# Two channels on the 128 contraction rows: a long convolution beside attention on one core

## The chip, the core and the metric

The kernel runs on one core of a Trainium2 chip. The core has five engines with instruction streams of their own: TensorE (PE in the profile) multiplies matrices, VectorE (DVE) and ScalarE (ACT) work element by element, GpSimd (POOL) and SyncE (SP) here mostly clear memory and start transfers (DMAs). They wait for each other by semaphores only. Matmuls write to PSUM, which has eight banks of 128 x 512 float32 values; everything else lies in SBUF, 128 partitions wide.

The metric is the time of one execution on the device in microseconds. The kernel before takes 828.38 us, the median of three runs (827.64 to 830.67). A profile is one further execution; its page and its trace are what the prediction is read from.

## What is computed

Two independent parts share one launch, and their outputs stand side by side.

```python
def _A_ref(x, wqkv, wo):                 # x: 1 x 2048 x 512, H = 32 heads of Dh = 16
    qkv = (x @ wqkv).reshape(B, S, 3, H, Dh)
    q, k, v = ...
    scores = einsum("bhqd,bhkd->bhqk", q, k) * (Dh ** -0.5)
    o = einsum("bhqk,bhkd->bhqd", softmax(scores), v)
    return o.reshape(B, S, D) @ wo

def _B_ref(q, k, v, shift_k, ssm_k, ssm_D):   # each 1 x 2048 x 512
    k_shift = sum over t < 4 of k delayed by 3 - t times shift_k[:, 3 - t]
    kv = k_shift * v
    y = causal convolution of kv with ssm_k along S, channel by channel
    return q * (y + kv * ssm_D)

return concatenate([_A_ref(...), _B_ref(...)], axis=-1)
```

In the source the convolution is written with Fourier transforms. The kernel computes it as matrix products.

## The kernel before

**Attention.** The scores are worked through in 2048 blocks of 128 keys by 512 queries. One step of the main loop (index `T`) takes two or three blocks into PSUM banks (`qk_mm`, L728), and one instruction of ScalarE writes their exponentials to `PT` (`emit_exp`, L761). One block of some steps goes to VectorE instead, which computes the exponential in four passes (`exp_on_dve`, L803, L810 twice, L815) into `PTD`. Two steps later the value matmuls (`emit_pv`, L844) add the blocks into bank `PVB` = 6, in four groups of 32 columns of the PE array, one for each pair of heads. When a group of heads is complete, VectorE turns and normalises it (`finish_group`). The order of everything is written out in Python before launch by a planner with assumed durations: `emit_qk`, `pv_step`, `emit_bg` and `warm_up` are called in turn for each `T`, and each piece of other work is put into a step only if it is expected to end before ScalarE needs its next scores (`MARGIN`). On the device each engine just follows its list.

**Convolution.** `kv` is computed by matmuls with diagonal taps (L468) and multiplied by `v` on VectorE into the tile `KV` (L514): 128 positions on the partitions, then groups of four channels, 16 blocks of positions, and the four channels. The filter `ssm_k` is reversed and padded, stored to `kz_scratch` in device memory (`kz_store`), and read back so that each partition holds the filter shifted by one more position: a row of `WR` is such a 128 x 2048 matrix of one channel, 512 KB per load (`load_wr`, L997, issued by SP). `WR` has `R_W` = 16 rows, which makes four slots of four channels. For four channels `conv_lags` runs 16 lags; in each, four matmuls with 128 moving columns go to the four groups of 32 columns of the array (L1014). The stationary operand of lag n is the 16 - n blocks of `KV` that this distance reaches. The results of 16 channels fill bank `BGB` = 7; VectorE copies them to half of `YB` (L1028), and after 32 channels `conv_turn` transposes them on PE (8 transposes, L1039) and VectorE multiplies by `q` in the tile `QN` (L1048). When 256 channels are done, `QN` is written out.

**The planner's rules for this work.** Nothing of the convolution starts before step `N_OPEN`; until then the units listed in `early` run, the `kv` units of the first 256 channels among them. Later units (`jobs`) have due times. `emit_bg` puts up to `LAGS` lags into a step if the room before ScalarE's next need allows it, if their filter is expected to have landed `WAIT` earlier, and if the block of instructions that PE is fetching is expected in time: the class `Tensor` counts 256 instruction words per block and assumes that the next block lands `FETCH` after the previous border is crossed. Where a step leaves PE free, `warm_up` adds filler matmuls with zero weights (`ZW`, L1219).

**On the other queues.** POOL clears constants and tiles at the start (L392 to L403), selects the diagonal taps (L560), clears pads (L387), and then starts the transfers of `QT`, `QN` and the outputs. SP starts the input transfers, the store of the filters and all filter loads, in order: a load that waits for its slot holds those behind it.

Of the kernel before, what the change touches and what calls it, by code (L numbers as in the profile page):

```python
# [9 lines left out]
U16 = mybir.dt.uint16  # L10

# [13 lines left out]
NB = S // 128  # L25
PAD = 128
# [3 lines left out]
R_W = 16  # L30
# [6 lines left out]
N_OPEN = 66  # L37
LAGS = 7
PACE = 1.4
# [21 lines left out]
T_DVE = 6  # L61
SLOT = 16
OPEN = 80
CLOSE = 12
REST = 2
# [5 lines left out]
S_C = 0.3  # L71
PLAN = 710
# [6 lines left out]
TAIL_GAP = 4  # L79
# [6 lines left out]
DMA_KB = 394  # L86
X_KB = 200
WINDOW = 3.4
HALF = 0.25
TURN = 0.2  # L90
# [4 lines left out]
FILL_GAP = 0.2  # L95
# [3 lines left out]
LATE = 0.2  # L99
# [8 lines left out]
FETCH = 6.3  # L108
# [111 lines left out]
def bass_concat_heads__mha_block__ssm_conv_h3__prompt_kernel(  # L220
# [36 lines left out]
    KV = sb("KV", [128, C // 4, NB, 4])  # L257
# [143 lines left out]
    h_va1 = pool.op(lambda e: e.memset(VA[:, :, :, 8 * VW:VROW].rearrange("p s k e -> p (s k) e"), 1.0))  # L401
    h_qt0 = pool.op(lambda e: e.memset(QT[:, 1:R_Q, :, :].rearrange("p r n f -> p (r n f)"), 0.0), us=(1.5, 1.6))
# [87 lines left out]
    def evac_unit(u, bank, h):  # L490
        kind = u[0]
        if kind == "q":
            p = u[1]
            last = [qk_done[2 * (p - R_Q) + i] for i in range(2)] if p >= R_Q else []
            hh = urgent(lambda e: e.tensor_scalar(QS[:, :], PS[:, bank, :], QSCALE, None, ALU.mult),
                        [h] + [h_q[2 * (p - 1) + i] if p > 1 else None for i in range(2)], us=V512)
            for par in range(2):
                for r0 in range(16 * par, 128, 32):
                    h_q[2 * p + par] = dma(pool, d_qs[p % 2][par], QT[r0:r0 + 16, p % R_Q, par, :], QS[r0:r0 + 16, :],
                                           [hh, h_qt0] + last, kb=16)  # L500
        elif kind == "k":
            _, o, sc = u
            c0 = KEYS0 if (o, sc) == (0, 0) else 0
            hh = urgent(lambda e: e.tensor_copy(KTo[:, o % 2, sc * 512 + c0:(sc + 1) * 512], PS[:, bank, c0:512]),
                        [h, qk_done[LAST[o - 2]] if o > 1 else None], us=(0.335, 0.46) if c0 else V512)
            h_k[(o, sc)] = hh
            if (o, sc) == (3, 3):
                load_wop(h)
        elif kind == "kv":
            _, c, i = u  # L510
            dst = KV[:, 32 * c:32 * c + 32, NB - 4 - 4 * i:NB - 4 * i, :]
            val = VST[c][:, NB - 4 - 4 * i:NB - 4 * i, :].rearrange("p b (k c) -> p k b c", c=4)
            src = PS[:, bank, :].rearrange("p (b k c) -> p k b c", b=4, c=4)
# [471 lines left out]
    h_yb = [None]  # L985
# [4 lines left out]
    def load_wr():  # L990
        while wr_free and wr_next[0] < C // 4:
# [10 lines left out]

    def conv_lags(qd, n0, n1):
        kk = qd % 8
        deps = [h_wr[qd], h_kvc[qd // 32]]
        r = 4 * wr_slot[qd]
        if kk % 4 == 0 and n0 == 0:
            deps.append(bank_free[BGB])

        def fn(e):  # L1010
            ins = None
            for n in range(n0, n1):
                for c in range(4):
                    ins = e.matmul(PS[32 * c:32 * c + NB - n, BGB, 128 * (kk % 4):128 * (kk % 4) + 128],  # L1014
                                   lhsT=KV[:, qd, n:NB, c],
                                   rhs=WR[:, r + c, 128 * (NB - 1 - n):128 * (NB - n)],
                                   start=(n == 0), stop=(n == NB - 1), tile_position=(0, 32 * c))
            return ins
        h = pe.op(fn, deps, run=LAG * (n1 - n0), kind="C", lat=0.4)
        if n1 == NB:  # L1020
            wr_free.append((wr_slot[qd], h))
            load_wr()
            if kk % 4 == 3:
                half = kk // 4
# [3 lines left out]
                hh = urgent(lambda e: e.tensor_copy(YB[:, half, :].rearrange("p (k i) -> p k i", k=4), src),  # L1028
                            [h, h_yb[0]], slack=S_C, us=V512)
                bank_free[BGB] = h_ybw[0] = hh  # L1030
        return h

    def conv_turn(b, bank):
        pbf = PS[:, bank, :].bitcast(BF16)

        def fn(e):
            ins = None
            for k in range(8):
                ins = e.transpose(pbf[:, 128 * k:128 * k + 128], YB[:, k // 4, 128 * (k % 4):128 * (k % 4) + 128],  # L1039
                                  IDN[:, :])  # L1040
            return ins
        h = pe.op(fn, [bank_free[bank], h_ybw[0], h_idn], run=0.445, kind="F")
        h_yb[0] = h
        sl = b // 8
        yv = pbf.rearrange("p (c j) -> p c j", j=32)[:, :, 0:NB].rearrange("p c j -> p j c")
        yv = bass.AP(tensor=yv.tensor, offset=pbf[:, NB - 1:NB].offset, ap=[yv.ap[0], [-1, NB], [32, CHB]])
        qv = QN[:, :, CHB * (b % 8):CHB * (b % 8) + CHB]
# [11 lines left out]
    units = [("kv", c, i) for c in range(2) for i in range(4)] + [(x, 1, i) for i in range(4) for x in "kv"]  # L1059
# [10 lines left out]
    state = {"qd": 0, "lag": 0, "turn": False, "started": False, "lags": 0.0, "left": C // 4 * NB, "t": 0.0}  # L1070
# [6 lines left out]
    def next_unit(T):  # L1077
        if T < N_OPEN:
            return early[0] if early and ready(early[0][1]) else None
        if state["turn"]:  # L1080
            return T, ("turn", state["qd"] // 8 - 1)
        return next((j for j in jobs if ready(j[1])), None)
# [5 lines left out]
    def unit_step(T):  # L1088
# [7 lines left out]
        while not tight:  # L1096
# [23 lines left out]
            us = pe.turn("F") + (0.445 if u[0] == "turn" else 0.478 if u[0] in ("kv", "v") else 2 * MM) + SWITCH  # L1120
# [22 lines left out]
    def emit_bg(T):  # L1143
# [5 lines left out]
        if T - end[0] in tail_mm:  # L1149
            assert st["qd"] == C // 4 and not st["turn"], (T, st)  # L1150
# [3 lines left out]
        if st["qd"] == C // 4 and not st["turn"]:  # L1154
# [3 lines left out]
        if st["turn"] and st["qd"] == C // 4:  # L1158
# [11 lines left out]
        while left > 0 and st["qd"] < wr_next[0] and kv_n[st["qd"] // 32] == 4 and at(h_wr[st["qd"]]) + WAIT <= pe.t:  # L1170
            if st["turn"] and st["qd"] % 4 == 3 and st["lag"] + left >= NB:
                left = NB - 1 - st["lag"]
# [5 lines left out]
            n1 = min(n0 + left, NB)  # L1178
# [4 lines left out]
            st["lag"] = n1 % NB  # L1183
            if n1 == NB:
                st["qd"] += 1
                if st["qd"] % 4 == 0:
                    st["turn"] = st["turn"] or st["qd"] % 8 == 0
                    break

    def filler_place(limit):  # L1190
# [5 lines left out]
        if state["started"] and state["lag"]:  # L1196
            return BGB, 0, NB, 128 * (state["qd"] % 4), 1, False
# [53 lines left out]
    assert state["qd"] == C // 4 and not state["turn"] and not jobs and not part[0], (state, jobs)  # L1251
# [65 lines left out]
```

## Time and profile before

| | |
|---|---|
| median of 3 runs | 828.38 us (827.64 to 830.67) |
| profiled execution | 828.52 us, span of its instructions 826.8 us |
| exponentials on ScalarE (L761) | 722 instructions, 804.1 us busy |
| exponentials on VectorE (L803, L810, L815) | 277 blocks, four instructions each |
| convolution matmuls (L1014) | 8192, 201.6 us busy |
| filler matmuls (L1219) | 498, 132.2 us busy |
| filter loads (WR<-kz_scratch) | 512 of 512 KB, median 8.4 us to landing |
| all transfers | 291.41 MB, mean 352 GB/s |

Busy time is the share in which an engine had an instruction running, matmuls and weight loads being pipelined over each other. In lists of waits, "issue" is idle time for which the profile shows nothing that the engine waited for. A line of the timeline gives start, duration, engine, source line, operation, output<-input, the number of merged instructions, and in brackets the idle time before and what ended it. A line of a table by stretches gives the stretch and its length, then busy time and number of instructions of PE, weight loads, DVE, ACT and POOL, the granted clock of PE (1.00 is full), the DMA share, and GB/s. A line of transfers by window ends with their number, the size of one, and the median us from issue to landing. A line of waits gives total us, number, and the longest.

### The profile page before, as it was taken

What the parts mean: (1) busy time and instruction counts of PE and PEld (TensorE: products, weight loads), DVE (VectorE), ACT (ScalarE), POOL (GpSimd) and SP (SyncE); (2) the same over time, 40 slices, a digit from 0 to 9 for tenths busy, and PEclk for the clock granted to TensorE, in tenths of its full rate; (3) what the DMA queues carried; (4) which work ended last, traced back from release to release, by engine and by line L of the source; (5) the groups of instructions that cost most, each with busy time, mean ns of one, the idle gap of its engine ahead of it and who ended that gap; (6) DMA issues with size and microseconds to landing.
All of it is one profiled execution on the core that took longest, in us unless ns stands there. A gap on an engine that the chain in (4) does not pass through costs nothing.

```text
span 826.8 us, 30549 instructions
## 1 busy us (share of the span) xinstructions
PE 762.2 (92%) x13603; PEld 324.2 (39%) x13642; DVE 794.2 (96%) x1360; ACT 807.0 (98%) x727; POOL 78.7 (10%) x155
## 2 busy tenths in 40 slices
PE   8998989999999899999899999999999999998987
PEld 3343434443333344444333344444433333333332
DVE  4999999999999899999999999999999999999985
ACT  6999999999999899999999999999999999999987
POOL 3300320010100101001011010101002002010000
PEclk9999999999999999999999999999999999999999
DMA  9998499999999999999999899999999999999922
GB/s 220 233 300 304 151 382 404 385 379 407 393 407 405 394 401 389 405 354 367 394 388 391 318 372 383 394 408 387 408 407 352 378 393 362 399 382 367 375 83 77
DMA packets 109235, 291.41 MB, mean 352 GB/s; under 512 B 37680, under 2 KB 41648, under 8 KB 108720
## 3 DMA queue, kind: packets, MB, share of 16 engines
q1 hardware_dynamic: 102256, 280.80, 90.8%
q0 software_dynamic: 5648, 8.27, 3.1%
q8 instruction: 108, 1.77, 0.9%
q10 hardware_dynamic: 1200, 0.39, 0.2%
q14 instruction: 23, 0.19, 0.1%
HBM read 276.83 MB, written 6.42 MB: 343 GB/s over the span
## 4 chain that ended last, share of the span: by engine, by line
ACT 77%; DVE 10%; PE 9%; issue 2%; DMA 1%; SPq 0%
ACT PT L761 77%; DVE EH L810 4%; PE PS L728 3%; DVE FX L803 2%; PE PS L1014 2%; PE PS L844 2%; DVE PTD L815 2%; PE PS L1219 1%; PE PS L468 1%; DMA xT<-in_A_x_dram 1%; DVE DT L905 0%; DVE YB L1028 0%; SPq L312 0%; DVE KV L514 0%; DVE OTN L925 0%
## 5 line engine op out<-in xcount | busy, mean ns | idle before, releaser
L761 ACT ACTIVATE PT<-PS 128x1024 bf16<-128x1024 f32 (+2 forms) x722 | 804.1, 1376 | 8.8 <-PE PS L728 8.3
L728 PE MATMUL PS<-QT,KTo 32*128 32x512 bf16 x2048 | 287.1, 385 | 38.7 <-ACT PT L761 14.1
L844 PE MATMUL PS<-PT,VA 128*32 128x512 bf16 x1771 | 199.7, 391 | 6.6 <-issue 3.5
L1014 PE MATMUL PS<-WR,KV 128*12 128x128 bf16 (+15 forms) x8192 | 201.6, 220 | 4.4 <-issue 4.3
L803 DVE TENSOR_SCALAR FX<-PS 128x512 f32<-128x512 f32 x277 | 187.9, 682 | 8.3 <-PE PS L728 8.0
L815 DVE SCALAR_TENSOR_TENSOR PTD<-EH,FX 128x512 uint16<-128x512 f32 x277 | 185.7, 677 | 0.0
L810 DVE SCALAR_TENSOR_TENSOR EH<-EH 128x512 f32<-128x512 f32 x277 | 185.4, 680 | 0.0
L810 DVE SCALAR_TENSOR_TENSOR EH<-FX 128x512 f32<-128x512 uint16 x277 | 184.5, 682 | 0.1
L1014 PEld LDWEIGHTS PS<-WR,KV 128*12 128x12 bf16 (+15 forms) x8192 | 140.6, 88 | 71.9 <-issue 42.5
L728 PEld LDWEIGHTS PS<-QT,KTo 32*128 32x128 bf16 x2048 | 73.3, 91 | 237.8 <-ACT PT L761 178.9
L1219 PE MATMUL PS<-IDN,ZW 128*32 128x512 bf16 (+3 forms) x498 | 132.2, 334 | 0.0
L312 POOL DMA_DIRECT2D QT<-QS x120 | 59.2, 501 | 483.7 <-DVE DR L912 133.7
L844 PEld LDWEIGHTS PS<-PT,VA 128*32 128x32 bf16 x1771 | 48.0, 93 | 114.0 <-issue 97.5
L844 PE MATMUL PS<-PTD,VA 128*32 128x512 bf16 x277 | 83.1, 383 | 0.0
L1219 PEld LDWEIGHTS PS<-IDN,ZW 128*32 128x32 bf16 x498 | 41.8, 96 | 24.1 <-issue 10.4
L905 DVE STREAM_TRANSPOSE DT<-PS 128x512 f32<-128x512 f32 x32 | 22.7, 709 | 7.3 <-PE PS L844 6.8
L1028 DVE CAST YB<-PS 128x512 bf16<-128x512 f32 x32 | 21.9, 684 | 1.4 <-PE PS L1219 1.1
L844 PEld LDWEIGHTS PS<-PTD,VA 128*32 128x32 bf16 x277 | 20.4, 95 | 1.6 <-DVE PTD L815 0.2
L955 PE MATMUL PS<-WKV,OTN 128*128 128x512 bf16 x53 | 16.9, 383 | 2.1 <-issue 1.6
L479 PE MATMUL PS<-WKV,xT 128*128 128x128 bf16 x256 | 18.1, 220 | 0.1
L456 PE MATMUL PS<-xT,WKV 128*128 128x512 bf16 (+1 forms) x52 | 15.0, 373 | 2.9 <-issue 1.1
L447 PE MATMUL PS<-xT,WQ 128*128 128x512 bf16 x45 | 14.4, 382 | 2.4 <-issue 2.1
(65 smaller groups left out, 209.2 us busy)
## 6 DMA issues: line engine op xcount, KB each, us to landing
WR<-kz_scratch SPq DMA_DIRECT2D x512, 512.0 KB, 8.4
kz_scratch<-WR SPq DMA_DIRECT2D x1, 2176.0 KB, 8.3
QN<-in_B_q_dram POOLq DMA_DIRECT2D x2, 1024.0 KB, 12.4
out_dram<-QN POOLq DMA_DIRECT2D x2, 1024.0 KB, 8.6
QT<-QS POOLq DMA_DIRECT2D x120, 16.0 KB, 5.3
out_dram<-OUTA POOLq DMA_DIRECT2D x12, 128.0 KB, 5.2
QN<-in_B_ssm_k_dram SPq DMA_DIRECT2D x1, 1024.0 KB, 8.3
OTN<-in_B_ssm_k_dram SPq DMA_DIRECT2D x1, 1024.0 KB, 9.2
```

Source lines behind the costliest of these rows:

```text
L312: f(outp, inp).then_inc(dsem.sem, 16)
L479: ins = e.matmul(PS[:, bank, 128 * j:128 * j + 128], lhsT=xT[:, dc, (4 * sc + j) * 128:(4 * sc + j + 1) * 128], rhs=WV[:, dc, o * 128:(o + ...
L728: ins = e.matmul(PS[:, bank, :], lhsT=KTo[32 * s:32 * s + 32, OF[n_] % 2, kt * 128:(kt + 1) * 128], rhs=QT[32 * s:32 * s + 32, n_ // 2 % R ...
L761: h_exp[T] = act.op(lambda e: e.activation(PT[:, p0:p0 + n, :].rearrange("p b f -> p (b f)"), PS[:, banks[0]:banks[0] + n, :].rearrange("p ...
L803: h_f = urgent(lambda e: e.tensor_scalar(fx, PS[:, bank, :], FIX_ADD, FIX_HI, ALU.add, ALU.min), [h, h_last.get(i - R_FX)], slack=S_FX)
L810: st["h"] = dve.op(lambda e: e.scalar_tensor_tensor(eh, src, (P1, P2)[j], src, ALU.add, ALU.mult), [st["h"], h_last.get(i - R_EH)], us=us)
L815: lambda e: e.scalar_tensor_tensor(out16, eh, P3, fx, ALU.mult, ALU.add),
L844: ins = e.matmul(dst, lhsT=w, rhs=rhs, start=(k == 0), stop=(k == KT - 1), tile_position=(0, 32 * s))
L905: h_t = urgent(lambda e: e.transpose(out=dt, in_=PS[:, PVB, :]), [h, h_mul.get(n - 1)], slack=S_T, us=(0.63, 0.751))
L1014: ins = e.matmul(PS[32 * c:32 * c + NB - n, BGB, 128 * (kk % 4):128 * (kk % 4) + 128], lhsT=KV[:, qd, n:NB, c], rhs=WR[:, r + c, 128 * (NB ...
L1028: hh = urgent(lambda e: e.tensor_copy(YB[:, half, :].rearrange("p (k i) -> p k i", k=4), src), [h, h_yb[0]], slack=S_C, us=V512)
L1219: pe.op(lambda e, s=s, k=k, rhs=rhs, bank=bank, rows=rows, c0=c0, first=first: e.matmul(PS[32 * s:32 * s + rows, bank, c0:c0 + 128 * k], l ...
```

## The change

Two channels, 64 apart, share the 128 contraction rows with 64 positions each. `KV` now holds, for 64 groups of eight channels, two parities and 32 half blocks of 64 positions; each product with `v` is done by four VectorE instructions on 64 partitions, and the half blocks that belong to the other channel's rows are zeros, cleared once by a memset on POOL ahead of those of `QT` and `WR`. One load brings the filters of two channels, 64 shifts each. A group of eight channels takes 32 lags of 64 positions, four matmuls each; the stationary operand has up to 32 columns. `WR` has 8 rows: two slots. Bank `BGB` now holds 32 channels when four groups are done; they go to one half of `YB` by one copy, and `conv_turn` has four transposes. The `kv` units of the second 128 channels move from the opening to steps 68 to 80. A number of the planner's constants change.

```diff
-R_W = 16
+R_W = 8
-N_OPEN = 66
-LAGS = 7
-PACE = 1.4
+N_OPEN = 64
+KV1 = 4
+LAGS = 6
+PACE = 1.2
-T_DVE = 6
+T_DVE = 4
-OPEN = 80
+OPEN = 100
-REST = 2
+REST = 4
-S_C = 0.3
-PLAN = 710
+S_C = 0.4
+PLAN = 720
-TAIL_GAP = 4
+TAIL_GAP = 3
-TURN = 0.2
+TURN = 0.1
-FILL_GAP = 0.2
+FILL_GAP = 0.25
-LATE = 0.2
+LATE = 0.1
-FETCH = 6.3
+FETCH = 5.0
...
-    KV = sb("KV", [128, C // 4, NB, 4])
+    KV = sb("KV", [128, C // 8, 2, 2 * NB, 4])
...
+    h_kv0 = pool.op(lambda e: e.memset(KV[:, :, :, :, :].rearrange("p o r u g -> p (o r u g)").bitcast(U32), 0), us=(8.8, 8.9))
...
-            h_kvc[c] = hh = urgent(lambda e: e.tensor_tensor(dst, src, val, ALU.mult), [h, h_vn[c]], us=V512)
+            for half in range(2):
+                for ch in range(2):
+                    hs, cs = slice(64 * half, 64 * half + 64), slice(64 * ch, 64 * ch + 64)
+                    dst = KV[cs, 16 * c:16 * c + 16, 1 - half, q0 + ch:q0 + 8:2, :].rearrange("p o q g -> p q o g")
+                    h_kvc[c] = hh = (dve.op if half or ch else urgent)(
+                        lambda e, dst=dst, hs=hs, ch=ch: e.tensor_tensor(dst, src[hs, :, ch], val[hs, :, ch], ALU.mult),
+                        [h, h_vn[c], h_kv0], us=(0.335, 0.46))
...
-            for c in range(4):
-                src = bass.AP(tensor=kz_ap.tensor, offset=kz_ap[4 * qd + c, 0].offset, ap=[[1, 128], [1, S]])
-                h_wr[qd] = dma(sp, d_wr[i], WR[:, 4 * i + c, :], src, [h_kzw[0], dep])
+            for g in range(4):
+                row = 128 * (qd // 16) + 4 * (qd % 16) + g
+                src = bass.AP(tensor=kz_ap.tensor, offset=kz_ap[row, 0].offset, ap=[[64 * LKZ, 2], [1, 64], [1, S]])
+                h_wr[qd] = dma(sp, d_wr[i], WR[:, 4 * i + g, :], src, [h_kzw[0], dep], kb=512)
...
+    DIST = [0, -1] + list(range(1, NLAG - 1))
...
-                for c in range(4):
-                    ins = e.matmul(PS[32 * c:32 * c + NB - n, BGB, 128 * (kk % 4):128 * (kk % 4) + 128],
-                                   lhsT=KV[:, qd, n:NB, c],
-                                   rhs=WR[:, r + c, 128 * (NB - 1 - n):128 * (NB - n)],
-                                   start=(n == 0), stop=(n == NB - 1), tile_position=(0, 32 * c))
+                d = DIST[n]
+                w = 64 if d < 0 else 128
+                for g in range(4):
+                    kv = KV[:, qd, (1 + d) % 2, (1 + d) // 2 * 2:2 * NB, g]
+                    ins = e.matmul(PS[32 * g:32 * g + 2 * ((30 - d) // 2 + 1), BGB, 128 * kk:128 * kk + w],
+                                   lhsT=kv, rhs=WR[:, r + g, S - 64 * d - 128:S - 64 * d - 128 + w],
+                                   start=(n == 0), stop=(n == NLAG - 1), tile_position=(0, 32 * g))
...
-            for k in range(8):
-                ins = e.transpose(pbf[:, 128 * k:128 * k + 128], YB[:, k // 4, 128 * (k % 4):128 * (k % 4) + 128],
-                                  IDN[:, :])
+            for k in range(4):
+                ins = e.transpose(pbf[:, 128 * k:128 * k + 128], YB[:, b % 2, 128 * k:128 * k + 128], IDN[:, :])
...
-    units = [("kv", c, i) for c in range(2) for i in range(4)] + [(x, 1, i) for i in range(4) for x in "kv"]
+    units = [("kv", 0, i) for i in range(4)] + [(x, 1, i) for i in range(4) for x in "kv"]
...
+    jobs += [(N_OPEN + KV1 + 4 * i, ("kv", 1, i)) for i in range(4)]
```

More of the change, by code (lines that the diff above doesn't have):

```diff
@@ L990, in load_wr @@
     def load_wr():
-        while wr_free and wr_next[0] < C // 4:
+        while wr_free and wr_next[0] < C // 8:
             (i, dep), qd = wr_free.pop(0), wr_next[0]
@@ L1001, in load_qn @@
                       q2[:, 256 * i:256 * i + 256].rearrange("(t p) d -> p t d", p=128), deps, kb=1860)
+    DIST = [0, -1] + list(range(1, NLAG - 1))
     def conv_lags(qd, n0, n1):
-        kk = qd % 8
-        deps = [h_wr[qd], h_kvc[qd // 32]]
+        kk = qd % 4
+        deps = [h_wr[qd], h_kvc[qd // 16]]
         r = 4 * wr_slot[qd]
-        if kk % 4 == 0 and n0 == 0:
+        if kk == 0 and n0 == 0:
             deps.append(bank_free[BGB])
@@ L1028, in conv_lags @@
                 hh = urgent(lambda e: e.tensor_copy(YB[:, half, :].rearrange("p (k i) -> p k i", k=4), src),
-                            [h, h_yb[0]], slack=S_C, us=V512)
+                            [h, h_yb[half]], slack=S_C, us=V512)
                 bank_free[BGB] = h_ybw[0] = hh
@@ L1067, in bass_concat_heads__mha_block__ssm_conv_h3__prompt_kernel @@
     jobs += [(step(9 + 7 * c) - 8, ("kv", c + 2, i)) for c in range(2) for i in range(4)]
+    jobs += [(N_OPEN + KV1 + 4 * i, ("kv", 1, i)) for i in range(4)]
     jobs += [(step(25 + 2 * qb) + 8 * t, ("op", qb, t)) for qb in range(NQB - 1) for t in range(4)]
     jobs.sort(key=lambda j: j[0])
-    state = {"qd": 0, "lag": 0, "turn": False, "started": False, "lags": 0.0, "left": C // 4 * NB, "t": 0.0}
+    state = {"qd": 0, "lag": 0, "turn": False, "started": False, "lags": 0.0, "left": C // 8 * NLAG, "t": 0.0}
     part = [None]
@@ L1119, in unit_step @@
                 free = max(free, at(*unit_deps(u)) + 0.13)
-            us = pe.turn("F") + (0.445 if u[0] == "turn" else 0.478 if u[0] in ("kv", "v") else 2 * MM) + SWITCH
+            us = pe.turn("F") + (0.223 if u[0] == "turn" else 0.478 if u[0] in ("kv", "v") else 2 * MM) + SWITCH
             lim = at(h_exp[T]) - 0.47 - MARGIN
@@ L1149, in emit_bg @@
         if T - end[0] in tail_mm:
-            assert st["qd"] == C // 4 and not st["turn"], (T, st)
+            assert st["qd"] == C // 8 and not st["turn"], (T, st)
             for t, g in tail_mm[T - end[0]]:
@@ L1153, in emit_bg @@
             return
-        if st["qd"] == C // 4 and not st["turn"]:
+        if st["qd"] == C // 8 and not st["turn"]:
             if T < end[0] + min(tail_mm) and h_wop[0] is not None:
@@ L1157, in emit_bg @@
             return
-        if st["turn"] and st["qd"] == C // 4:
+        if st["turn"] and st["qd"] == C // 8:
             if T < end[0] + min(tail_mm) - 1 and at(h_ybw[0]) > pe.t - 0.2:
@@ L1169, in emit_bg @@
         left = min(LAGS, int(st["lags"]), int((room(T) - pe.turn("C") - SWITCH) / LAG), int(pe.spare() / 8))
-        while left > 0 and st["qd"] < wr_next[0] and kv_n[st["qd"] // 32] == 4 and at(h_wr[st["qd"]]) + WAIT <= pe.t:
-            if st["turn"] and st["qd"] % 4 == 3 and st["lag"] + left >= NB:
-                left = NB - 1 - st["lag"]
+        while left > 0 and st["qd"] < wr_next[0] and kv_n[st["qd"] // 16] == 4 and at(h_wr[st["qd"]]) + WAIT <= pe.t:
+            if st["turn"] and st["qd"] % 4 == 3 and st["lag"] + left >= NLAG:
+                left = NLAG - 1 - st["lag"]
                 if left <= 0:
@@ L1182, in emit_bg @@
             conv_lags(st["qd"], n0, n1)
-            st["lag"] = n1 % NB
-            if n1 == NB:
+            st["lag"] = n1 % NLAG
+            if n1 == NLAG:
                 st["qd"] += 1
                 if st["qd"] % 4 == 0:
-                    st["turn"] = st["turn"] or st["qd"] % 8 == 0
+                    st["turn"] = True
                     break
@@ L1250, in bass_concat_heads__mha_block__ssm_conv_h3__prompt_kernel @@
         T += 1
-    assert state["qd"] == C // 4 and not state["turn"] and not jobs and not part[0], (state, jobs)
+    assert state["qd"] == C // 8 and not state["turn"] and not jobs and not part[0], (state, jobs)
     assert not early_dve and not flow and not acts and not dves
```

32 lines of the change are left out of this document (17 added, 15 removed).

## The prediction

> **What bounds the kernel now.** I read the page's busy times first, then the waits by engine, then stretches of 1 us around the longest waits, then the order of work inside two of them, and the transfers by window last.
>
> ```profile
> span 826.8 us, 30549 instructions
> ...
> PE 762.2 (92%) x13603; PEld 324.2 (39%) x13642; DVE 794.2 (96%) x1360; ACT 807.0 (98%) x727; POOL 78.7 (10%) x155
> ...
> q1 hardware_dynamic: 102256, 280.80, 90.8%
> ...
> q8 instruction: 108, 1.77, 0.9%
> ```
>
> ScalarE (ACT) is busy for all but 19.8 us. Of those, 7.9 lie before its first exponential and 7.1 behind the last (start of the first and end of the last in the timeline). What a change can win inside the loop is therefore the rest, and the list of ACT's waits says who owns it:
>
> ```profile
> ACT PT L761 <- PE PS L728: 8.3, 12, 2.1
> ```
>
> Twelve waits for scores from TensorE (PE), the longest 2.1 us; 1.3 us of them lie in the first 11 us. Where ACT's busy time falls short of the stretch (the windows of 20 us): 0.42 at 100 to 120, 1.09 at 220 to 240, 2.07 at 260 to 300, 0.58 at 340 to 360, 0.11 at 640 to 660, 2.56 at 780 to 800. Together 6.8 us. Each follows a standstill of PE:
>
> ```profile
> 222.41 0.22 PE L1014 MATMUL PS<-WR,KV 128*9 128x128 bf16 x1
> ...
> 223.82 0.57 PE L1014 MATMUL PS<-WR,KV 128*9 128x128 bf16 x27 [1.19 <-issue]
> ...
> 228.91 0.34 PE L1014 MATMUL PS<-WR,KV 128*5 128x128 bf16 x11
> ...
> 229.97 0.33 PE L1014 MATMUL PS<-WR,KV 128*3 128x128 bf16 x9 [0.72 <-issue]
> ```
>
> A run of 28 convolution matmuls breaks off after one and goes on 1.19 us later; between this break and the next lie 126 recorded matmuls. The instruction queue moved 1.77 MB in 108 packets, 16.4 KB each, and 27,245 PE instructions over 108 is 252, or some 126 matmuls with their weight loads. So PE stood still because the next block of its own program had not arrived. Counting 128 matmuls back from each break gives the time a block took from the earlier boundary to the restart: 5.8, 6.7, 6.2, 8.2, 6.6 and 8.7 us (breaks at 105, 222, 229, 278, 355 and 787 us). The standstills (1.13, 1.19, 0.72, 1.75, 0.19, 0.99, 0.60, 1.98) sum to 8.55 us and cost ACT the 6.8: 0.8 us per us. The two longest also cost the clock:
>
> ```profile
> 281.00:282.00 1.00, 1.00 (x9) 0.22 (x11) 0.28 (x1) 1.00 (x2) 0.00 (x0) 0.61 1.06 422
> 282.00:283.00 1.00, 1.00 (x33) 0.79 (x25) 1.00 (x3) 0.74 (x1) 0.00 (x0) 0.50 1.05 418
> 283.00:284.00 1.00, 1.00 (x8) 0.23 (x8) 1.00 (x3) 0.13 (x1) 0.00 (x0) 0.50 1.06 414
> ```
>
> In the last three columns the granted clock is 0.50 while the DMA share is 1.05. The DMA engines are full because of the filter loads, and that delays small transfers. The same 16 KB transfer (QT<-QS), first in 80 to 100 us, where the DMA share is 0.33, then in 160 to 240 us, where it is 1.02:
>
> ```profile
> QT<-QS POOLq DMA_DIRECT2D x8, 16.0 KB, 3.2
> ...
> QT<-QS POOLq DMA_DIRECT2D x16, 16.0 KB, 5.3
> ```
>
> [...]
>
> **The change, part by part.**
> *ACT.* In the changed instruction order the exponentials are 406 of two blocks, 317 of three, 2 of four (before 398, 321, 3): 1771 blocks in both, and VectorE (DVE) has 277 in both. A block costs 417 ns (1605 - 1188, means of the three- and two-block forms); 804.1 busy less 1771 x 0.417 leaves 65.6 us over 722, 0.09 each. Three more instructions: +0.3 us, on the path.
> *Filter loads.* 256 instead of 512 of 512 KB: 134 MB less, and 256 issues fewer on SP. DMA is busy 5.3 us (2.1 MB at 395 GB/s) of each 11.7 (750 us over 64 pairs-of-four) where it was full. A block of program should then come sooner. Bounds: by 0, or by the whole 2.1 us of the 16 KB rows. On a line between those rows (0.33 share, 3.2; 1.02, 5.3) a share of 0.55 gives 1.4 less. From 6.5 us, the middle of the measured times, that is 5.1; since loads still come in bursts I take 5.4.
> *The order around the blocks.* A faster refill matters only against how fast PE eats a block. I cut both PE orders every 128 matmuls and counted score matmuls in each piece, 0.396 us each (811.8 us of exponentials over 2048). Pieces below 6 us: 6 of 106 before, 25 of 106 after; the changed planner packs tighter (its refill constant is 5.0 for 6.3, LAGS 6 for 7). If every refill took F, PE would stand still for, in all: before 7.4 us at F = 6.5 (seen 8.55); after 0.5 at 5.0, 2.2 at 5.5, 8.5 at 6.0, 13.5 at 6.2, 22.5 at 6.5. At 5.4 about 2.0, and ACT loses 0.8 x 2.0 = 1.6 in place of 6.8: -5.2 us.
> *Convolution on PE.* 2048 lags of four matmuls in both, 256 matmuls of them only 64 wide. A lag takes 57 ns (the seven lags from 221.29 to the filler at 221.69 us). The weights have up to 32 columns for 16. Rows:
>
> ```profile
> L1014 PEld LDWEIGHTS PS<-WR,KV 128*1 128x1 bf16 x512 | 13.7, 83 | 5.3 <-issue 1.6
> ...
> L1014 PEld LDWEIGHTS PS<-WR,KV 128*16 128x16 bf16 x512 | 14.6, 93 | 9.8 <-issue 7.7
> ...
> 221.06 0.10 PEld L844 LDWEIGHTS PS<-PT,VA 128*32 128x32 bf16 x3 [0.23 <-issue]
> ```
>
> One column 83 ns, 16 columns 93, and 32 columns of the value matmuls 93 as well; three of those, for three column groups, lie within 0.10 us, so they run beside each other. Cost 0 if that holds; else the rival below. [...]
> *Other PE work.* 64 transposes and 39 fillers fewer. Off the path: PE has 65 us of idle time besides its fillers.
> *DVE.* 32 operations of 512 columns go (16 YB copies, 16 KV products, spaced 0.60), 64 of 256 columns on 64 partitions come. Bounds for one: 0.30 (half of 0.60) to 0.395 (three 256-wide L599 in 1.27 us). At 0.35, +3.2 us. DVE idles 32.6 us; the planner places these. Nothing on the path; without that cover up to 6.1 us.
> *Zeroing KV on POOL.* 8192 words: 7.2 us by elements (2048 in 1.79), 14.3 at most by bytes. Moved behind it are the QT and WR memsets and DG's select. POOL was idle 9.9 us before that select (15.3 us); QT is needed at 30.1, WR at 39.8, DG at 44. Cost 0.
> *Two buffer slots for four.* A slot is refilled while the other is used. From the end of its use to the next in PE's order: at least 10.7 us, median 12.7 (before 13.9 and 19.0). Loads landed in 6.1 us (80 to 100 us) to 8.4. Cost 0, 2.3 us to spare. KV's second 128 channels come later, so the first lags are fewer (138 for 192 in the first 75 us), but the last lag lies at score block 2016 in both: the tail stays.
>
> **Sum.** +0.3 - 5.2 = -4.9. The profiled execution took 828.52 us (span 826.8 and 1.7 around it), 0.14 above the median, 828.38. Forecast 828.38 - 4.9 = 823.5; with F from 5.0 to 5.7 and the last small waits, 821.3 to 825.5.
>
> **Rivals.**
> *Two kinds of refill (same).* Refills that start inside a burst (5.3 of 11.7 us, 46%) still take 6.5, others 4.4. Then 0.46 x 22.5 = 10.4 us of standstill, ACT loses 8.3 for 6.8: 830.2. For it: the break at 355 us took 6.6 with DMA partly free (0.54 to 0.66 in its last 3 us). Against: a burst is four loads, not an endless queue.
> *Refills no faster (slower).* Place: the 34 pieces under 6.5 us. 22.5 x 0.8 = 18.0 for 6.8, +0.3: 839.9. It turns at F = 5.95, where the after column passes 7.4 and the packing eats the gain. Against: the 3.2 us row.
> *Weight loads in line (slower).* If the four loads of a lag follow each other at the slope (93 - 83)/15 = 0.67 ns a column, a lag takes 2.67 ns per column, over 57 ns from 22 columns up (28 ns at 32 columns): 180 ns summed over the 32 lags, 64 times, 11.5 us, 9.2 of it at ACT: 823.5 + 9.2 = 832.7. Against: the 0.10 us row.
> *Refill isn't the cause.* Then only +0.3: 828.7. Against: the breaks lie a block apart.
> *It doesn't do what it says.* Filters land late in the two slots and PE waits for DMA: if by 1 us in each of 64 turns x 0.8 = 51 us: 880.
>
> **Chances.** Forecast 0.56, two kinds 0.16, no faster 0.13, weight loads 0.07, not the cause 0.05, late filters 0.03. Half a per cent, 4.1 us, is what a measurement here can tell (runs 827.64 to 830.67). Faster means below 824.2: 0.53 of the forecast's 0.56. Slower means above 832.5: 0.13 + 0.07 + 0.03 = 0.23. Same 0.24. The range 820.5 to 836 leaves out most of "no faster" and late filters, and a little below.
>
> **What would show it.** Right: DMA mean near 190 GB/s; ACT's waits for L728 near 3 us in place of 8.3; breaks in runs of convolution matmuls mostly under 0.5 us; granted clock 1.00 throughout; QT<-QS landing under 5. Wrong: "issue" standstills more numerous than eight (packing); runs of 24 matmuls with 32-column weights longer than 0.50 us (weight loads); PE waiting for DMA WR (slots); DVE waits before FX that PE did not cause.

## The result and the profile after

The changed kernel takes 2703.81 us (median of four runs, 2703.10 to 2704.48); the kernel before, run beside it, 829.52 us (827.64 to 830.96). The ratio is 3.260 (95% interval 3.252 to 3.268). The forecast was 823.5 us, the range 820.5 to 836: wrong, and far outside.

From the page of the changed kernel: span, busy times, granted clock and DMA share in 40 slices, all packets, and the queue with the filter loads (packets, MB, share of 16 engines' span).

```profile
span 2702.4 us, 30121 instructions
...
PE 881.7 (33%) x13498; PEld 365.6 (14%) x13539; DVE 814.2 (30%) x1392; ACT 831.8 (31%) x730; POOL 84.5 (3%) x156
...
PEclk9866566556656666656656656656656656666667
DMA  7111111111111111111112111111111111111111
...
DMA packets 68784, 157.13 MB, mean 58 GB/s; under 512 B 30000, under 2 KB 33968, under 8 KB 68272
...
q1 hardware_dynamic: 61808, 146.55, 14.0%
```

The bytes halved, as they should (291 MB to 157). But the DMA engines are nearly idle, and so is everything else. The list of waits (total us, number, longest) says what everybody waits for:

```profile
ACT PT L772 <- PE PS L739: 1855.6, 211, 34.2
PEld PS L1031 <- DMA WR<-kz_scratch: 1787.6, 64, 34.4
PE PS L1031 <- DMA WR<-kz_scratch: 1768.8, 64, 34.1
```

PE waits for a filter load 64 times, once in each turn of four loads, some 28 us on average. Before, no such wait stood among PE's. ACT waits behind it, because the next score matmuls stand in PE's list after the convolution. One such wait in the middle, in the timeline of PE and in the table by stretches:

```profile
1018.88 0.23 PE L1031 MATMUL PS<-WR,KV 128*2 128x128 bf16 x4
1050.22 0.36 PE L1031 MATMUL PS<-WR,KV 128*32 128x128 bf16 x8 [31.11 <-DMA WR<-kz_scratch]
```

```profile
1020.00:1040.00 20.00, 0.00 (x0) 0.00 (x0) 1.50 (x3) 0.01 (x1) 0.00 (x0) 0.52 0.13 52
```

In these 20 us PE does nothing; the DMA share is 0.13 and 52 GB/s are moved. Something is late while the engines that could bring it are idle for seven eighths of their time. 0.13 is 2/16: read as two engines at work, each moves 26 GB/s, about what one of 16 does in the kernel before (395/16 = 24.7). The chain of waits shows the same from SP's side (start, us, what):

```profile
997.24 9.78 SPq L316
1007.02 0.04 issue
1007.06 9.78 SPq L316
1016.84 0.04 issue
1016.89 33.29 DMA WR<-kz_scratch
```

One load of 512 KB drains in 9.8 us; the waits of 33.29 us in the chain start at 1016.89 and 1096.73, two turns apart, so a turn takes 39.9 us (4 x 512 KB at 53 GB/s is 39.6). 64 x 39.92 = 2555 us; the opening, with its first convolution matmul at 97.8 us, and the end are the rest.

The small packets fit this. Those under 512 B fall from 37680 to 30000, by 7680. If each engine that takes part in a load adds one small packet (the author's assumption), 512 loads on 16 engines make 8192 and 256 loads on two make 512: the difference is 7680.

### The profile page after: what moved, and what is told of

It reads as the page before. It is cut to its first block, busy times and chain, and to the rows that moved or that the text cites. A ratio compares the mean times of both kernels' runs of the same rounds, so it can differ in the third digit from the quotient of the medians.

```text
span 2702.4 us, 30121 instructions
## 1 busy us (share of the span) xinstructions
PE 881.7 (33%) x13498; PEld 365.6 (14%) x13539; DVE 814.2 (30%) x1392; ACT 831.8 (31%) x730; POOL 84.5 (3%) x156
## 3 DMA queue, kind: packets, MB, share of 16 engines
q8 instruction: 107, 1.75, 0.3%
## 4 chain that ended last, share of the span: by engine, by line
SPq 47%; DMA 36%; PE 9%; ACT 5%; DVE 3%; issue 1%
SPq L316 47%; DMA WR<-kz_scratch 36%; ACT PT L772 5%; PE PS L739 3%; PE PS L1031 2%; PE PS L855 2%; DVE EH L821 1%; PE PS L1234 1%; DVE FX L814 1%; DVE PTD L826 0%; PE PS L473 0%; DVE KV L524 0%; PE PS L484 0%; DMA xT<-in_A_x_dram 0%; PE PS L452 0%
## 5 line engine op out<-in xcount | busy, mean ns | idle before, releaser
L772 ACT ACTIVATE PT<-PS 128x1024 bf16<-128x1024 f32 (+2 forms) x725 | 828.8, 1232 | 1858.6 <-PE PS L739 1855.6
L1031 PE MATMUL PS<-WR,KV 128*24 128x128 bf16 (+8 forms) x8192 | 257.9, 259 | 1768.8 <-DMA WR<-kz_scratch 1768.8
L1031 PEld LDWEIGHTS PS<-WR,KV 128*32 128x32 bf16 (+7 forms) x8192 | 175.4, 108 | 1877.4 <-DMA WR<-kz_scratch 1787.6
L739 PE MATMUL PS<-QT,KTo 32*128 32x512 bf16 x2048 | 331.9, 444 | 24.6 <-ACT PT L772 4.9
L855 PE MATMUL PS<-PT,VA 128*32 128x512 bf16 x1771 | 223.4, 443 | 5.9 <-DVE DT L916 5.2
L855 PE MATMUL PS<-PTD,VA 128*32 128x512 bf16 x277 | 94.3, 440 | 0.0
L1234 PEld LDWEIGHTS PS<-IDN,ZW 128*32 128x32 bf16 x459 | 41.8, 105 | 22.8 <-issue 11.7
L537 DVE CAST VA<-PS 128x512 bf16<-128x512 f32 x16 | 11.0, 685 | 62.6 <-PE PS L484 62.6
L1062 DVE TENSOR_TENSOR QN<-PS,QN 128x512 bf16<-128x512 bf16 x16 | 11.0, 688 | 59.1 <-PE PS L1055 59.0
L974 DVE CAST OUTA<-PS 128x512 bf16<-128x512 f32 x12 | 8.2, 687 | 62.7 <-PE PS L966 62.6
L500 DVE TENSOR_SCALAR QS<-PS 128x512 bf16<-128x512 f32 x15 | 10.3, 686 | 37.3 <-PE PS L452 37.2
```

The lines of the kernel that those rows point to most:

```text
L739: ins = e.matmul(PS[:, bank, :], lhsT=KTo[32 * s:32 * s + 32, OF[n_] % 2, kt * 128:(kt + 1) * 128], rhs=QT[32 * s:32 * s + 32, n_ // 2 % R ...
L772: h_exp[T] = act.op(lambda e: e.activation(PT[:, p0:p0 + n, :].rearrange("p b f -> p (b f)"), PS[:, banks[0]:banks[0] + n, :].rearrange("p ...
L855: ins = e.matmul(dst, lhsT=w, rhs=rhs, start=(k == 0), stop=(k == KT - 1), tile_position=(0, 32 * s))
L1031: ins = e.matmul(PS[32 * g:32 * g + 2 * ((30 - d) // 2 + 1), BGB, 128 * kk:128 * kk + w], lhsT=kv, rhs=WR[:, r + g, S - 64 * d - 128:S - 6 ...
L1234: pe.op(lambda e, s=s, k=k, rhs=rhs, bank=bank, rows=rows, c0=c0, first=first: e.matmul(PS[32 * s:32 * s + rows, bank, c0:c0 + 128 * k], l ...
```

## The experiments

The theories are named by a letter in the expectations: A, the source pattern `[[64 * LKZ, 2], [1, 64], [1, S]]` has 2 as its first count, and that count decides how many engines take part; B, the two far-apart regions of memory are slow; C, two slots are too few. The others are told where they come up. The kernel before was run beside each group; its medians there lie between 826.54 and 829.16 us.

**Is it the count, the addresses, or the slots?** `e1_split` brings the two channels by one load each:

```diff
-src = bass.AP(..., ap=[[64 * LKZ, 2], [1, 64], [1, S]])
-h_wr[qd] = dma(sp, d_wr[i], WR[:, 4 * i + g, :], src, ..., kb=512)
+for ch in range(2):
+    src = bass.AP(..., offset=kz_ap[row + 64 * ch, 0].offset, ap=[[1, 64], [1, S]])
+    h_wr[qd] = dma(sp, d_wr[i], WR[64 * ch:64 * ch + 64, 4 * i + g, :], src, ..., kb=HALF_KB)
```

> The changed kernel with each filter load issued as two loads of 64 partitions (one per channel); the same bytes from the same addresses to the same places. Theory A (a load whose source has a first dimension of 2 is moved by 2 of the 16 DMA engines): each half has a first dimension of 64, all 16 engines work, DMA share well above 0.13, no wait for the filters, and the time falls from 2703 us to what the prediction had without it, 821 to 836 us. Theory B (the two address regions, 278 KB apart, are slow to read): the addresses are the same, still above 2000 us. Theory C (two slots are too few to hide a load): the slots are the same, so PE still waits at most of the 64 turns, above 1500 us.

`e5_slots3` has a third slot (`R_W = 12`) and the load as it was:

> The changed kernel with 12 rows of filters, so three slots instead of two. Theory A: two DMA engines move 134 MB at about 53 GB/s, 2540 us, however many slots there are: 2600 to 2720 us. Theory C: with one more load ahead a third or more of the waiting goes, below 2100 us. Theory B: as A.

`e2_outer2` and `e2_outer16` leave the kernel before as it is, and write its load of one channel with a first count of 2 and of 16. `e2_outer8` came later, with 8. The moved bytes stay 512 KB per load.

```diff
-ap=[[1, 128], [1, S]]
+ap=[[63, 2], [1, 64], [1, S]]     # e2_outer2
+ap=[[7, 16], [1, 8], [1, S]]      # e2_outer16
+ap=[[15, 8], [1, 16], [1, S]]     # e2_outer8
```

> The kernel before with each filter load's source written with 2 x 64 rows instead of 128, the second 64 rows starting one element early (so that the two dimensions are not merged; half of each filter matrix is shifted by one position, and the output is not the reference's). The same 512 KB from the same 4 KB neighbourhood as before, four slots. Theory A: 512 loads x 512 KB at 53 GB/s, 5070 us, so 4900 to 5500 us. Theory B: no second region, so as before, 829 us. Theory C: four slots, so as before, 829 us.

> As the one with 2 x 64, but 16 x 8 rows, each group starting one element earlier per group than before (output not the reference's). Theory A: 16 engines, as before, 825 to 835 us; if three dimensions or the overlap alone were slow, it would be far above that.

> As the kernel before with 2 x 64 rows, but 8 x 16 rows (output not the reference's). Theory A: 8 engines, 512 loads of 512 KB at 8 x 24.7 = 198 GB/s at best, 1360 us and the opening, so 1380 us; more, up to 1700, if the eight crowd on the same ports.

Measured: `e1_split` 866.85 us (862.41 to 872.06), 1.046 [1.039, 1.053] times before; `e5_slots3` 2686.6; `e2_outer2` 5221.64; `e2_outer16` 1006.83; `e2_outer8` 1421.62. C falls with the third slot: 17 us of 1874. B falls with `e2_outer2`: neighbouring addresses, and the kernel before becomes six times slower by the source pattern alone. It is the first count and not the third dimension: `e2_outer16` has three counts too and takes 1006.83. From the pages of `e2_outer2` and then of `e2_outer8`:

```profile
DMA packets 102067, 291.39 MB, mean 56 GB/s; under 512 B 30512, under 2 KB 34480, under 8 KB 101552
...
q1 hardware_dynamic: 95088, 280.77, 13.5%
```

```profile
DMA packets 105139, 291.40 MB, mean 205 GB/s; under 512 B 33584, under 2 KB 37552, under 8 KB 104624
...
q1 hardware_dynamic: 98160, 280.78, 50.7%
```

Shares of 13.5% (2/16 is 12.5) and 50.7% (8/16 is 50), and small packets fewer by 7168 = 512 x (16 - 2) and 4096 = 512 x (16 - 8). Dividing each page's MB by share times span, all 16 engines would have moved 398 and 390 GB/s, against 374 before: so read, each engine that takes part runs at no less than its pace of before, and the others get nothing. The dose fits A. The upper end expected of `e2_outer8`, 1700 us, supposes crowded ports, which no run shows: eight engines ran at 24.4 GB/s each (390/16) where 24.7 were expected, and the time lies 3% above the 1380 us.

Two things missed. `e2_outer16` was expected at 825 to 835; its small packets, 37680 as before, count 16 engines, but at a share of 94.5% only 290 GB/s were moved, so that PE waited 126 us for filters. And `e1_split` was slower than its 821 to 836.

**What the split left over.** Theory P: a load into 64 consecutive partitions runs slower, whatever else; O: it is the number of transfers. On the kernel before, whose order and bytes stay as they are, `e6_halfparts` splits each load by partitions and `e6_halfcols` by columns.

```diff
-src = bass.AP(tensor=kz_ap.tensor, offset=kz_ap[4 * qd + c, 0].offset, ap=[[1, 128], [1, S]])
-h_wr[qd] = dma(sp, d_wr[i], WR[:, 4 * i + c, :], src, [h_kzw[0], dep])
+for ch in range(2):                       # e6_halfparts
+    src = bass.AP(..., offset=kz_ap[4 * qd + c, 0].offset + 64 * ch, ap=[[1, 64], [1, S]])
+    h_wr[qd] = dma(sp, d_wr[i], WR[64 * ch:64 * ch + 64, 4 * i + c, :], src, ..., kb=256)
+for ch in range(2):                       # e6_halfcols
+    s0 = S // 2 * ch
+    src = bass.AP(..., offset=kz_ap[4 * qd + c, 0].offset + s0, ap=[[1, 128], [1, S // 2]])
+    h_wr[qd] = dma(sp, d_wr[i], WR[:, 4 * i + c, s0:s0 + S // 2], src, ..., kb=256)
```

> The kernel before, same order on PE, each filter load issued as two of 64 partitions. Theory P: 268 MB at 200 to 245 GB/s, so 1150 to 1400 us. Rival O (it is the number of transfers that costs, not where they go): as slow as the next one, whatever that is. If neither holds: 829 us.

> The kernel before, same order on PE, each filter load issued as two of 128 partitions and half the columns: as many transfers of the same size as the one before. Theory P: all partitions are reached, 825 to 850 us. Rival O: as slow as the one with 64 partitions, above 1100 us.

Measured 1100.23 and 843.60 us. Against the 827.36 us beside them, twice the transfers by columns cost 16 us, split by partitions 273; P, though below its lower end of 1150. Whether it is the 64 neighbouring partitions or only that a load has 64 rows in place of 128 was not separated. From the table by stretches of `e6_halfparts`, then of `e1_split`:

```profile
400.00:420.00 20.00, 14.54 (x237) 6.30 (x232) 13.47 (x23) 14.03 (x13) 0.00 (x0) 0.83 1.03 244
```

```profile
200.00:220.00 20.00, 17.35 (x382) 8.04 (x374) 19.50 (x34) 19.20 (x18) 1.07 (x3) 1.00 1.04 243
```

The share is full (1.03, 1.04) at 244 and 243 GB/s, where the kernel before has 390 to 407 in the windows of 20 us from 200 to 300 us. So the share of busy engines does not tell their pace: here it is some 0.61 of that of before, and no run shows why. `e1_split` needs half the bytes and still has 70% of the engines' time, and PE waits 13.7 us in ten waits for filters and 9.6 us in twelve for nothing shown (4.3 in seven before).

**Was the prediction's own gain real?** Theory R: PE stands still for late blocks of its program because filter loads fill the DMA engines. `e4_halfbytes` is the kernel before with half of each filter load left out from the second use of a slot on, and the same order on every engine (the convolution reads old columns).

```diff
+w = S if qd < R_W // 4 else S // 2
-src = bass.AP(..., ap=[[1, 128], [1, S]])
-h_wr[qd] = dma(sp, d_wr[i], WR[:, 4 * i + c, :], src, ...)
+src = bass.AP(..., ap=[[1, 128], [1, w]])
+h_wr[qd] = dma(sp, d_wr[i], WR[:, 4 * i + c, 0:w], src, ...)
```

> The kernel before, same order on every engine, but from the second use of each slot on a filter load brings only the first half of its columns, so 256 KB; the convolution's output is wrong. Theory R (late program blocks stop PE because the filter loads fill the DMA engines, the base of the prediction): mean DMA about 190 GB/s, ACT's waits for L728 fall from 8.3 us to 1 to 3, time 821 to 825 us. Rival (the standstills have another cause, or halving the load does not shorten a refill): waits stay near 8 us, 827 to 831 us.

Measured 820.55 us (819.68 to 823.54) against 827.36; 0.992 [0.989, 0.994]. The list of waits and the list of transfers of `e4_halfbytes`:

```profile
ACT PT L761 <- PE PS L728: 4.3, 6, 1.1
```

```profile
QT<-QS POOLq DMA_DIRECT2D x120, 16.0 KB, 3.5
```

Half the waits of before (8.3, 12), at a mean of 196 GB/s. The time lies just under the expected 821 to 825, and the 4.3 us of waits above the expected 1 to 3. PE's own waits say why, before and then in `e4_halfbytes`:

```profile
PE PS L1014 <- issue: 4.3, 7, 1.2
PE PS L844 <- issue: 3.5, 3, 2.0
...
PE PS L728 <- DVE PTD L815: 1.7, 1, 1.7
```

```profile
PE PS L728 <- DVE PTD L815: 2.0, 1, 2.0
...
PE PS L844 <- issue: 1.3, 1, 1.3
```

Six of the prediction's eight standstills are gone or down to 0.15 us, and for these R holds. The arrival of a block is in no trace: that they were late blocks is read from this fall, from the 126 recorded matmuls between two breaks, and from the 252 instructions for each packet of the instruction queue; that a block has 256 words and that its time runs from the border before it are the planner's assumptions. Two stay as long as they were: at 106 us 1.30 us (1.13 before), at 279 us 2.02 (1.75 before); together they cost ACT 3.0 us. At the second the profile names a VectorE instruction, but in PE's list the place lies 886 weight loads, seven blocks of the prediction's 126, behind the standstill at 230 us, so it too is read as a late block. Its block was due while the loads of one turn kept the DMA share at 1.01 and 1.08 (270 to 274 us), and took 8.9 us by the same count. So read, a refill that met a burst stayed slow here even with half the bytes, as the rival "Two kinds of refill" has it.

The lighter DMA is worth 6.8 us (4.7 to 9.2 by the interval) to the order of before. The profiled execution, 823.54 us, was the slowest of the six, and in it ACT's waits fall by 4.0.

**What of the changed order itself?** `e7_splitquarter` is `e1_split` with a quarter of the columns loaded after the sixth group of eight channels, which takes the DMA load away. L is the prediction's rival of weight loads in line, V a loss on VectorE.

```diff
+w = S if qd < 6 else S // 4
-src = bass.AP(..., ap=[[1, 64], [1, S]])
+src = bass.AP(..., ap=[[1, 64], [1, w]])
```

> The split kernel of the first experiment with its own order, but after the first six groups each half load brings a quarter of its columns, 64 KB; the convolution's output is wrong. Theory P (a transfer into 64 consecutive partitions runs at about half rate, so the split kernel is held by DMA): no wait for the filters, refills in time, 821 to 830 us, which is what the rest of the change costs. Rival L (weight loads of up to 32 columns run in line and slow PE by about 11 us): 832 to 840 us. Rival V (VectorE, with four products in place of one, holds ACT up): ACT still waits 15 us or more, above 840 us.

Measured 838.18 us (836.41 to 838.32), 1.012 [1.009, 1.015]. P's range, up to 830, was missed, and V's 15 us of waits nearly met (13.4). The time falls into L's range for another reason: convolution matmuls with 18 to 30 columns of weights take as long as with 2 to 8 (means of 220 to 223 ns against 219), and after 200 us ACT loses only some 1.8 us. The loss, 11 us, lies between 20 and 200 us: 3.1 behind one full load that came late (PE waited 2.15 us for it before 138.7 us), 3.3 behind products into `KV`, the rest behind other VectorE work and one late block.

Two more tried to help the split form through the planner: `e8_told` is `e1_split` with the slower loads told to the planner and a third slot; `e9_told_late` is `e8_told` with VectorE's first exponential at step 6, as before the change. S: the split form stays slow in any plan.

```diff
-R_W = 8
+R_W = 12
-HALF_KB = 270
+HALF_KB = 430
-FETCH = 5.0
+FETCH = 6.3
...
-T_DVE = 4
+T_DVE = 6
```

> The split kernel with the planner told what the runs showed: a half load costs 1.09 us (430 for 270), a program block 6.3 us (FETCH, for 5.0), and three slots in place of two. Pieces of 128 matmuls shorter than 6 us: 5 (25 in the split kernel). Theory P (the split kernel's loss is half-rate loads and blocks packed too tight for full DMA engines, with a few us lost in the opening): no wait for filters, few standstills, 826 to 838 us. Rival S (the split form itself is slow in a way no plan mends): above 850 us.

> The one before it with VectorE's first exponential at step 6 in place of 4 (275 blocks on VectorE for 277). If the collision of VectorE's early exponentials with POOL's select near 16 us costs the opening 2 to 3 us: 2 us less ACT idle before 30 us, 1 to 2 us faster than its neighbour. If not: the same or 1 us slower, for two more blocks on ACT (0.8 us).

Measured 849.60 us (842.28 to 852.04) and 842.25 (839.56 to 843.08). `e8_told` met neither side. `e9_told_late` gains 7 where 1 to 2 were expected. Part of it is seen: from the timeline of ACT in `e9_told_late`,

```profile
7.91 38.40 ACT L772 ACTIVATE PT<-PS 128x2048 bf16<-128x2048 f32 x32 [1.04 <-PE PS L739]
```

ACT runs unbroken from 7.91 to 46.3 us, where `e8_told` breaks off four times between 18 and 27 us, 3.0 us in all, and starts 0.8 later. The later start is a difference between executions: `e4_halfbytes`, whose opening is that of before, starts its exponentials at 8.51 us. The rest of the 7 us is a difference between two plans and was not taken apart.

**The load mended in one line.** `e10_interleaved` is the changed kernel, its order and constants included, with the two outer counts of the source exchanged:

```diff
-ap=[[64 * LKZ, 2], [1, 64], [1, S]]
+ap=[[1, 64], [64 * LKZ, 2], [1, S]]
```

> The changed kernel with the two outer dimensions of each filter load's source exchanged: the 64 shifts outside, the two channels inside, so that one load still brings 512 KB to 128 partitions, but the filters of the two channels lie on alternate partitions. KV keeps its order, so the convolution's sums are not the reference's; the instructions and their order are those of the changed kernel. Theory A (engines follow the first dimension of the source: 64 can be spread over 16): no wait of TensorE for filters worth naming, share of the filter loads near half of the 90.8% of the kernel before if a 128-row load keeps its 395 GB/s, up to 65% if it runs at the 290 GB/s of the load of 16 x 8 rows, and QT<-QS landing in 3.5 to 4.5. The time then is that of the changed order itself without the defect: 826 to 838, since the order with quarter loads took 838 with full-size half-partition loads in its opening. If the prediction's sum was right but for the load's price, 821 to 826; if what the slow split loads left over (838 to 850) lies in the order and not in the loads (theory S), 838 to 846. If the load's rate depends on the number of rows that each outer step brings, and not on the number of engines (2 x 64 slow, 64 x 2 slower still), the time is above 2700.

Measured 834.38 us (831.22 to 835.84, seven runs) against 826.54; 1.0072 [1.0046, 1.0097]. From the page, the list of transfers, and PE's waits of `e10_interleaved`:

```profile
DMA packets 72368, 157.15 MB, mean 189 GB/s; under 512 B 33584, under 2 KB 37552, under 8 KB 71856
...
q1 hardware_dynamic: 65392, 146.56, 52.4%
```

```profile
WR<-kz_scratch SPq DMA_DIRECT2D x256, 512.0 KB, 5.8
...
QT<-QS POOLq DMA_DIRECT2D x120, 16.0 KB, 2.8
```

```profile
PE PS L739 <- DVE KV L524: 5.6, 10, 1.1
PE PS L739 <- DVE FX L814: 4.9, 13, 0.7
PE PS L1031 <- issue: 3.2, 4, 1.8
```

In the kernel before, no wait of PE for `KV` is listed, and for `FX` little:

```profile
PE PS L728 <- DVE FX L803: 0.9, 5, 0.2
```

Of the slowdown of 1874 us, 1869 go by this line. The small packets again count 16 engines (8192 - 256 x 16 = 4096 fewer than before), and no wait for filters is left. QT<-QS landed sooner than the 3.5 to 4.5 us expected. What remains, +0.7%, lies for the most part in VectorE's work, worked out in the next section.

## Why the prediction was wrong

**The step that failed** is "Filter loads", where it says that "DMA is busy 5.3 us (2.1 MB at 395 GB/s) of each 11.7". The bytes were halved rightly and the rate was carried over from a load with another access pattern. A turn of four loads took 39.9 us, not 5.3. "Two buffer slots for four" stands on landing times of the old pattern too ("Loads landed in 6.1 us (80 to 100 us) to 8.4") and was right in itself: with 5.8 us (`e10_interleaved`) two slots cause no wait.

The rival "it doesn't do what it says" named the mechanism, filters late and PE waiting for DMA WR, and gave it 0.03 and 1 us in each of 64 turns. It was about 28. The new pattern's first count, 2, stands in the diff; the prediction read the byte count and the number of issues in that line, and not the shape. What such a count costs is in no row of before; `e2_outer2`, the kernel before with that load alone changed, shows it (56 GB/s for 352).

**Bound and gain: right in the main.** ACT set the end, and PE's standstills, read as late program blocks, cost it the 6.8 us. The sum gave -5.2 for lighter DMA, and `e4_halfbytes` shows -6.8 on the order of before. In the mended kernel PE's standstills in the convolution and its fillers are 3.2 + 0.6 = 3.8 us against 8.55 (2.0 were forecast), and cost ACT 2.2 us at 255 us (1.20 and then 1.00) and 0.1 at 209, where before lost 6.8 and the forecast was 1.6. The granted clock was not 1.00 throughout, as forecast: 0.66 from 255 to 260 us. QT<-QS landed in 2.8 us ("under 5"), and the DMA mean was 189 GB/s ("near 190").

**"Nothing on the path" for VectorE: wrong**, hidden by the larger error. In `e10_interleaved` ACT is busy 809.0 us of 832.7, in the profile of before 807.0 of 826.8. The 5.9 us longer span (the medians lie 7.8 apart) is 2.0 of busy time (0.3 predicted; the rest was not taken apart), 3.8 of idle time in the first 80 us (10.45 for 6.63 by the windows of 20 us), -0.2 from 80 to 820 us (7.28 for 7.44), and 0.3 behind. In the middle stretch the refills gave 4.6 and all of it was eaten. One place shows by what; VectorE, PE and ACT in the timeline of `e10_interleaved`:

```profile
184.93 1.78 DVE L524 TENSOR_TENSOR KV<-PS,OUTA 64x256 bf16<-64x256 f32 x4
...
186.76 0.38 PE L739 MATMUL PS<-QT,KTo 32*128 32x512 bf16 x1 [0.78 <-DVE KV L524]
...
187.18 1.45 ACT L772 ACTIVATE PT<-PS 128x1536 bf16<-128x1536 f32 x1 [0.73 <-PE PS L739]
```

The next score matmul needs the bank that the product still reads; four products in a row take 1.78 us where one took 0.60, and ACT stands still for 0.73. The prediction priced a product at 0.35 us, between bounds of 0.30 and 0.395; it takes 0.42, above both, and VectorE's busy time rose by 10.3 us (794.2 to 804.5) where 3.2 were forecast and 6.1 the upper bound. It counted the sum of VectorE's work against VectorE's idle time, and not how long one unit holds its bank. Followed back from ACT in the same timeline, the idle time from 80 to 820 us is 2.3 us behind late blocks, 1.9 behind such products (seven waits), 0.8 in the two waits that follow the first of them at 112 us, 1.4 behind `FX` (four waits, two of them close behind products), 0.2 behind a copy into `YB`, and 0.7 that shows no cause. So VectorE took 4.2 us or so of the 4.6.

The 3.8 us of the opening have three parts. ACT's first exponential starts at 8.58 us for 7.91, which is no cost of the change (`e4_halfbytes` with the opening of before: 8.51). Between 53 and 63 us five waits, 1.6 us, follow PE's waits for products, of which this is the longest:

```profile
60.11 0.60 PE L461 MATMUL PS<-xT,WKV 128*128 128x512 bf16 x2 [1.32 <-DVE KV L524]
```

And the earlier first exponential on VectorE (step 4 for 6) meets POOL's selection of the taps. VectorE's two-input operation beside it, in the same timeline:

```profile
15.29 2.01 POOL L571 TENSOR_SCALAR_AFFINE_SELECT OTN<-SHK 128x2048 bf16<-128x2048 bf16 x1 [3.02 <-DMA SHK<-in_B_shift_k_dram]
...
15.72 2.13 DVE L821 SCALAR_TENSOR_TENSOR EH<-EH 128x512 f32<-128x512 f32 x1
```

2.13 us instead of 0.69. ACT then waits 2.1 us between 18 and 24 us; `e9_told_late`, with VectorE's first exponential at step 6, does not. Less the 0.6 us that ACT waited up to 80 us in the kernel before, the parts make 0.7 + 1.6 + 2.1 - 0.6 = 3.8.

**The other steps.** Zeroing KV on POOL took 6.92 us for the 7.2 worked out from elements, and held nothing up: `e9_told_late` has it too and starts its exponentials at 7.91 us as before. Convolution on PE, cost 0: right; loads of 32 columns have records of 110 ns against 93 for 16, and the matmuls run no slower (in `e10_interleaved` a run of 24 from 284.54 us, 30 columns at its start, takes 0.53 us, one from 189.01 us, 8 columns, 0.51; so the sign named for this rival, over 0.50 us, could not have told). Of the rivals on refills, "isn't the cause" falls with the six standstills that are gone in `e4_halfbytes`, and "no faster" with the 3.8 us of `e10_interleaved`, where it has 22.5. "Two kinds of refill" had the mechanism of the two that stayed, and its price too high: 834.38 is not evidence for its 830.2, since the remaining refills cost ACT 2.3 us and not 8.3.

## What to carry to other kernels

Price a changed DMA by its access pattern, its first count above all, before its bytes: first counts of 2 and 8 left the share at 13.5% and 50.7% here while PE waited for filters, and with 64 in place of 2 (`e10_interleaved`) no wait for filters was left. Check the DMA share against the GB/s: the share of 0.13 beside a wait of 31 us went with idle engines, not with a full memory, and shares of 1.03 and 1.04 moved 244 and 243 GB/s where the kernel before moves 390 to 407. For work that moves to another engine, ask how long each single piece holds what the critical engine needs next, besides whether the sum fits into idle time. No form of this change run here is faster than the kernel before: the best split one with whole loads takes 842.25 us, the mended load 834.38, and that one would still need `KV` in the order in which its filters lie; neither that nor a plan with fewer products in a row was tried.

## What the runs showed of the hardware

With all 16 engines at work, as the small packets count them, the pace still differed. MB over share times span, for the filter queue as a whole: 374 GB/s in the kernel before, 355 with half the columns per load, 336 for 64 x 2 rows (`e10_interleaved`), 296 for 16 x 8 rows (`e2_outer16`), 265 and 241 for 64 partitions (`e6_halfparts`, `e1_split`). Why 16 x 8 rows were slower than 128 in one count, no run shows. A small load beside the filters mostly landed sooner the less of the engines' time they took: QT<-QS landed in 2.0 us with the filter queue's share at 14% (the changed kernel), 2.8 at 52% (`e10_interleaved`), 5.3 at 91% (the kernel before); but 3.6 at 51% with eight engines (`e2_outer8`).

The granted clock was low during and after PE's idle time, as in the prediction's two stretches at 0.50: 0.52 in the 20 us shown above, 0.645 over the whole changed kernel, so that ACT's and VectorE's waits also include slower matmuls (score matmuls 444 ns in the mean of the changed kernel, 386 in `e10_interleaved`).
